# Local queries and keys of the second batch in their own buffers, and one packed product for the third Fourier row tile

## The chip, the cores and the metric

The kernel runs on one core of a Trainium2 chip. The metric is the device time of one execution in microseconds (us). TensorE (PE, with its weight loads as PEld), VectorE (DVE), ScalarE (ACT), GpSimd (POOL) and SyncE (SP) run side by side and wait for each other by semaphores. Most transfers are issued by SP, some by POOL and ACT, and all of them share 16 DMA engines. KB is 1024 bytes.

## The reference

Four batches of 576 tokens with 8 heads of 64 go through four steps, all in float32.

```python
scores = scale * q @ k.T              # heads 0-3: local mask, heads 4-7: strided mask, 32 each
attn = softmax(scores) @ v            # -> x of (4, 576, 512)
mixed = real(fft(fft(x, axis=1), axis=2))
u = x + mixed
x = u + relu(layernorm(u) @ w_ch1) @ w_ch2          # 512 -> 2048 -> 512
u = x + (relu(x.T @ w_tok1) @ w_tok2).T             # over tokens, 576 -> 256 -> 576
out = u + relu(u @ w_ch1b) @ w_ch2b                 # 512 -> 1536 -> 512
```

## The kernel before

**Attention.** The work is 24 groups, six per batch: three local ones (`"l"`, two query tiles of 96 each) and three strided ones (`"s"`). Each group has two halves (`e` = 0 and 1, one parity of heads). `Group.scores` (L193) starts a half with a mask product (L205) and adds the score products (L211). `softmax` (L217) reduces on DVE (L227) and takes exponentials on ACT (L230), `trans` (L234) transposes on PE, `av` (L245) multiplies by the values, and `out` (L257) scales on DVE and stores to the DRAM tensor `xd[b]` from SP (L271, L277, L278).

**Loads.** `load_qk(b, g, pool)` (L170) loads queries and keys of batch `b`, local (`g` = 0) or strided (`g` = 1). Queries go to `qz[g]`, one tile that serves all batches; half of its partitions were set to zero once (L517, L518), so that 128-row products give one head each. Keys go to `k{g}` with one buffer. A load of the next batch thus waits until the scores of the batch before have been taken. Batch 0 is loaded at the start (L514 to L521); the local part of the next batch is asked for at group 3 of each batch (L582), the strided part at its group 0 (L585). SP issues its transfers in one order, and a transfer waits for the eighth one before it on that queue.

**Fourier.** After group 2 of the next batch, `Fourier.load` (L287) fetches the rows of a batch from `xd` in three row tiles (`ST`, 128, 128 and 33 rows): `xa` holds rows from the front half, `xr` their partners from the back half. `prep` (L301) folds them on DVE into `e` (L312 to L316), and ACT and POOL split `e` into a high and a low float32r part in `f` (L317, L318). `s1` (L320) transforms along the tokens: five column tiles, each with high times high, high times low and low times high over the three row tiles, 9 products (6 for the last column). The third tile's rows above 33 are zeros. `s2` (L346) transforms along the channels, adds to `xa` and `xr` (L373) and stores both to `ud[b]` (L375, L376). `fft` (L560) says after which group each piece may go out. The first two batches' Fourier work lies among the attention groups; the third's ends after them, and the fourth's lies in the first steps of the MLP (`last_fft`, L635).

**After it.** `u_rows` (L445) loads token tiles of 128 rows from `ud` for the LayerNorm; the first three are asked for at group 17 (L602), their statistics (L471) at group 19. Then come the first MLP (`gemm1` L413, `gemm2` L432), the token mixer and the second MLP, all led by PE.

**Order.** Up to the second MLP no order is written out by hand: the framework's planner orders each engine's instructions at build, by dependencies, program order and the added hints (`behind`, L74). The constants (L530 to L542) are loaded by POOL's queue and wait for the first batch's strided values (L531).

Of the kernel before, what the change touches and what calls it, by code (L numbers as in the profile page):

```python
# [27 lines left out]
ST = [(0, 128), (128, 128), (256, 33)]  # L28
# [15 lines left out]
def attention_fourier_mlp_kernel(ctx: ExitStack, tc: tile.TileContext, a: dict, out: bass.AP):  # L44
# [118 lines left out]
    k_t, qz = {}, []  # L163
# [6 lines left out]
    def load_qk(b, g, pool):  # L170
        t = pool.tile([P, 2, S], F32, tag=f"k{g}", name="k", bufs=(1, 1)[g])
        k_t[b, g] = t
        for ps in ([slice(0, 1), slice(1, 2)] if b == 0 and g < 1 else [slice(0, 2)]):
            for e in range(2):
                r = slice(64 * e, 64 * e + 64)
                nc.sync.dma_start(out=qz[g][r, e, ps], in_=a["qt"][b, g, r, ps])
            nc.sync.dma_start(out=t[:, ps], in_=a["kt"][b, g, :, ps])
# [7 lines left out]
    class Group:  # L185
# [7 lines left out]
        def scores(self):  # L193
            self.sc, self.mm, self.red = [], [], []
            n, q, k = 2 * self.n, self.q, self.k
            for e in range(2):
# [9 lines left out]
                for i, t in enumerate(self.idx):  # L206
                    qs = slice(96 * t, 96 * t + 96) if self.kind == "l" else slice(SR[t], SR[t] + q)
                    ks = slice(LW[kv(t)], LW[kv(t)] + P) if self.kind == "l" else qs
                    for hp in range(2):
                        j = i * 2 + hp  # L210
                        last = nc.tensor.matmul(  # L211
                            out=sc[:q, j * k:(j + 1) * k], lhsT=qz[self.g][:, e, hp, qs],
                            rhs=k_t[self.b, self.g][:, hp, ks], start=False, stop=j == n - 1)
# [68 lines left out]
    class Fourier:  # L282
# [4 lines left out]
        def load(self, i):  # L287
            r0, n = ST[i]
# [3 lines left out]
            na = min(n, 288 - r0)  # L292
            if i == 2:
                nc.gpsimd.memset(xa[32:33], 0.0)
            if i == 0:
                nc.gpsimd.memset(xr[0:1], 0.0)
            nc.sync.dma_start(out=xa[:na], in_=xd[self.b][r0:r0 + na, :])
            for c0, c1 in ([(1, 16), (16, n)] if i == 0 else [(0, n)]):
                self.last = nc.sync.dma_start(out=xr[c0:c1], in_=xd[self.b][287 + r0 + c0:287 + r0 + c1, :])

        def prep(self, i, prev=None, prev2=None):  # L301
            r0, n = ST[i]
            f = self.f = self.k["f"]
# [13 lines left out]
            behind(nc.scalar.activation(out=f[:n, 0, i], in_=e[:n], func=AF.Copy), prev2)  # L317
            nc.gpsimd.tensor_tensor(out=f[:n, 1, i], in0=e[:n], in1=f32(f[:n, 0, i]), op=ALU.subtract)  # L318

        def s1(self, mt, prev=None):  # L320
            pm = ps_m("g")
            mats = []
            f = self.f
            w = self.k["ss" if mt in (2, 3) else "cs"]
            c = slice(128 * mt, 128 * mt + 128)
# [20 lines left out]
        def s2(self, i, prev=None):  # L346
            r0, n = ST[i]
            c = slice(r0, r0 + n)
# [25 lines left out]
            na = min(n, 288 - r0)  # L374
            nc.sync.dma_start(out=ud[self.b][287 + r0:287 + r0 + n, :], in_=xr[:n])  # L375
            nc.sync.dma_start(out=ud[self.b][r0:r0 + na, :], in_=xa[:na])  # L376
# [10 lines left out]
    class Mlp:  # L387
# [52 lines left out]
        def u_tile(self, c):  # L440
            if c % 3 < 2:
                return self.lp.tile([P, DM], F32, tag="u", name="u", bufs=6)
# [47 lines left out]
    if True:  # L490
# [37 lines left out]
        f = fp.tile([P, 2, 3, 512], F32R, name="f")  # L528
# [3 lines left out]
        for t in (g4[1], alt, f[:, 0, 2], f[:, 1, 2], cs[0][:, 2], cs[1][:, 2], ss[0][:, 2], ss[1][:, 2]):  # L532
            nc.gpsimd.memset(f32(t), 0.0)
        cons = tc.issue_after(tick.ins)
        cons.__enter__()
        for i in range(2):
            for t, w in ((cs[i], a["cs"][i]), (ss[i], a["ss"][i])):
                nc.gpsimd.dma_start(out=t[:, 0:2], in_=w[:, 0:2])
                nc.gpsimd.dma_start(out=t[:33, 2], in_=w[:33, 2])
# [39 lines left out]
        for gno, g in enumerate(gl):  # L579
            b, gi = g.b, g.gi  # L580
            if gi == 3 and b + 1 < B:
                load_qk(b + 1, 0, ap)  # L582
# [18 lines left out]
            if gno == 17:  # L601
                us = [u_rows(T, lp.tile([P, DM], F32, tag="u", name="u", bufs=6)) for T in range(3)]  # L602
            if gno == 21:
                us += [u_rows(T, lp.tile([P, DM], F32, tag="u", name="u", bufs=6)) for T in range(3, 6)]
# [223 lines left out]
        def u_load(T):  # L828
            u = lp.tile([P, DM], F32, tag="u", name="u", bufs=6)
# [211 lines left out]
        def finish(G):  # L1041
# [11 lines left out]
            def halves(t):  # L1053
                if G == Gs[-1]:
                    k = lp.tile([P, DM], F32, tag="u", name="k", bufs=6)
# [87 lines left out]
def _constants():  # L1143
# [15 lines left out]
    s = np.arange(289)  # L1159
    full = {}  # L1160
    for nm, f in (("cs", np.cos), ("ss", np.sin)):
        w = np.zeros((384, 290))
        w[:289, :289] = trig(f, 576, s, s)
        full[nm] = w.reshape(3, P, 290).transpose(1, 0, 2)
# [61 lines left out]
```

## Time and profile before

| what | us |
|---|---|
| median of 3 runs (lowest, highest) | 928.37 (926.74, 932.41) |
| the profiled execution | 922.47 |
| its span | 920.7 |
| PE busy, share of the span | 892.5, 97% |
| DVE, ACT, POOL busy | 560.0, 408.3, 313.0 |

The times are of whole executions; the profile is of one execution, and every row below is from it. Its span starts at its first instruction. Busy times of PE count pipelined matmuls whole, so that they overlap; a busy PE is not PE at its peak. The chain that ended last is 63% PE, 11% DVE and 9% DMA.

### The profile page before, as it was taken

What the parts mean: (1) busy time and instruction counts of PE and PEld (TensorE: products, weight loads), DVE (VectorE), ACT (ScalarE), POOL (GpSimd) and SP (SyncE); (2) the same over time, 40 slices, a digit from 0 to 9 for tenths busy, and PEclk for the clock granted to TensorE, in tenths of its full rate; (3) what the DMA queues carried; (4) which work ended last, traced back from release to release, by engine and by line L of the source; (5) the groups of instructions that cost most, each with busy time, mean ns of one, the idle gap of its engine ahead of it and who ended that gap; (6) DMA issues with size and microseconds to landing.
All of it is one profiled execution on the core that took longest, in us unless ns stands there. A gap on an engine that the chain in (4) does not pass through costs nothing.

```text
span 920.7 us, 15422 instructions
## 1 busy us (share of the span) xinstructions
PE 892.5 (97%) x5554; PEld 824.2 (90%) x5554; DVE 560.0 (61%) x1046; ACT 408.3 (44%) x1069; POOL 313.0 (34%) x372
## 2 busy tenths in 40 slices
PE   7989989999999999999999999999999999999997
PEld 6979988999998989998888897777899999999997
DVE  4667979798894434443443446645434444888774
ACT  5978776353442333233223224323455545444432
POOL 3122222332330133344444333422223001946660
PEclk9989999999999999999999999999999999999999
DMA  9997864234431354644744665579833287156351
GB/s 260 282 289 216 255 205 136 98 127 146 138 111 68 99 160 146 196 128 126 220 141 136 209 200 180 176 262 313 293 120 147 104 270 243 36 161 222 125 203 47
DMA packets 116972, 161.00 MB, mean 175 GB/s; under 512 B 9662, under 2 KB 70180, under 8 KB 116896
## 3 DMA queue, kind: packets, MB, share of 16 engines
q1 hardware_dynamic: 114928, 157.29, 54.0%
q0 software_dynamic: 1712, 2.51, 1.1%
q8 instruction: 44, 0.72, 0.3%
q14 instruction: 32, 0.26, 0.1%
q10 hardware_dynamic: 256, 0.21, 0.1%
HBM read 104.92 MB, written 55.06 MB: 174 GB/s over the span
## 4 chain that ended last, share of the span: by engine, by line
PE 63%; DVE 11%; DMA 9%; ACT 5%; issue 4%; POOL 4%; SPq 3%; POOLq 0%; DVEq 0%; ACTq 0%
PE oo L1036 14%; PE oo L432 10%; PE h L413 10%; PE z L895 8%; PE y L895 4%; DMA wraw<-in_w1b_dram 4%; POOL wt L147 3%; PE tu L806 3%; PE tk L784 3%; PE sc L211 2%; PE w L895 2%; SPq L101 2%; DVE wu L112 2%; DVE wu L108 2%; DVE wu L113 2%
## 5 line engine op out<-in xcount | busy, mean ns | idle before, releaser
L413 PE MATMUL h<-uT,wAh 128*128 128x384 f32 x768 | 203.1, 337 | 0.2
L413 PEld LDWEIGHTS h<-uT,wAh 128*128 128x128 f32 x768 | 139.0, 188 | 5.2 <-PE g L334 0.4
L1036 PE MATMUL oo<-wo,ht 128*128 128x256 f32 x972 | 133.7, 281 | 0.0
L413 PE MATMUL h<-uT,wAl 128*128 128x384 f32 x384 | 129.0, 336 | 0.0
L1036 PEld LDWEIGHTS oo<-wo,ht 128*128 128x128 f32 x972 | 126.5, 189 | 0.0
L432 PE MATMUL oo<-wAh,hh 128*128 128x512 f32 x288 | 113.9, 398 | 4.3 <-ACT hh L417 4.2
L432 PE MATMUL oo<-wAl,hh 128*128 128x512 f32 x288 | 113.7, 395 | 0.0
L432 PE MATMUL oo<-wAh,hl 128*128 128x512 f32 x288 | 104.4, 396 | 0.2 <-DVE hl L418 0.2
L418 DVE SCALAR_TENSOR_TENSOR hl<-h,hh 128x384 fp32r<-128x384 f32 x96 | 52.6, 552 | 76.0 <-ACT hh L417 75.8
L108 DVE TENSOR_SCALAR wu<-wu 128x512 f32<-128x512 f32 (+1 forms) x62 | 38.5, 622 | 78.2 <-ACT wu L106 73.2
L124 POOL TENSOR_TENSOR wAl<-wu,wAh 128x512 fp32r<-128x512 f32 x32 | 45.9, 1437 | 104.3 <-ACT wAh L123 104.3
L417 ACT ACTIVATE hh<-h 128x384 fp32r<-128x384 f32 x96 | 45.9, 484 | 70.4 <-PE h L413 68.9
L147 POOL TENSOR_TENSOR wt<-wu 128x128 f32<-128x128 f32 x48 | 21.1, 461 | 158.3 <-DVE wu L113 158.3
L413 PEld LDWEIGHTS h<-uT,wAl 128*128 128x128 f32 x384 | 72.1, 188 | 2.8
L432 PEld LDWEIGHTS oo<-wAh,hh 128*128 128x128 f32 x288 | 54.1, 188 | 15.6 <-ACT hh L417 6.6
L106 ACT ACTIVATE wu<-wraw 128x512 f32<-128x512 f32 (+1 forms) x62 | 41.0, 662 | 60.6 <-DMA wraw<-in_w1b_dram 46.9
L895 PE MATMUL z<-ut,wo 128*128 128x384 f32 x324 | 64.5, 338 | 1.7 <-DVE ut L863 1.7
L432 PEld LDWEIGHTS oo<-wAh,hl 128*128 128x128 f32 x288 | 53.8, 188 | 13.7 <-DVE hl L418 1.3
L432 PEld LDWEIGHTS oo<-wAl,hh 128*128 128x128 f32 x288 | 54.1, 188 | 8.9
L230 ACT ACTIVATE sm<-sc,st 96x128 f32<-96x128 f32 (+2 forms) x176 | 61.6, 373 | 0.6
L895 PEld LDWEIGHTS z<-ut,wo 128*128 128x128 f32 x324 | 56.4, 188 | 2.1 <-DVE ut L863 2.0
L211 PE MATMUL sc<-k,qz 128*96 128x128 f32 (+2 forms) x352 | 51.0, 283 | 5.3 <-DMA k<-in_kt_dram 5.3
(197 smaller groups left out, 1840.9 us busy)
## 6 DMA issues: line engine op xcount, KB each, us to landing
wo<-wsd SPq DMA_DIRECT2D x84, 256.0 KB
wsd<-wraw SPq DMA_DIRECT2D x24, 448.0 KB
wsd<-wbl SPq DMA_DIRECT2D x24, 448.0 KB
u<-u2d SPq DMA_DIRECT2D x36, 256.0 KB
hd<-hs SPq DMA_DIRECT2D x12, 768.0 KB
hw<-hd SPq DMA_DIRECT2D x36, 256.0 KB
wraw<-in_w1a_dram SPq DMA_DIRECT2D x16, 512.0 KB
wraw<-in_w2a_dram SPq DMA_DIRECT2D x16, 512.0 KB
```

The source lines that it names most:

```text
L106: behind(nc.scalar.activation(out=f32(u), in_=f32(high), func=AF.Abs, scale=2.0**16), relu.get("hh"))
L108: clamp = eng().tensor_scalar(f32(u), f32(u), E_MIN, E_MAX, op0=ALU.max, op1=ALU.min)
L124: nc.gpsimd.tensor_tensor(out=lo[:, :n], in0=u, in1=f32(hi[:, :n]), op=ALU.subtract)
L147: nc.gpsimd.tensor_tensor(out=o, in0=x, in1=y, op=ALU.add if plus else ALU.subtract)
L211: last = nc.tensor.matmul(out=sc[:q, j * k:(j + 1) * k], lhsT=qz[self.g][:, e, hp, qs], rhs=k_t[self.b, self.g][:, hp, ks], start=False, s ...
L230: self.exp = nc.scalar.activation(out=smv[:, j, :], in_=sc[:, j, :], func=AF.Exp, scale=SCALE, bias=st[:, 1, j:j + 1], accum_out=st[:, 2, ...
L413: nc.tensor.matmul(out=h[:, :384], lhsT=l[:, ws], rhs=r[:, kd, :], start=x == 0, stop=x == 11)
L417: relu["hh"] = nc.scalar.activation(out=hh, in_=h[:, :384], func=AF.Relu)
L418: relu["hl"] = nc.vector.scalar_tensor_tensor(out=hl, in0=h[:, :384], scalar=0.0, in1=f32(hh), op0=ALU.max, op1=ALU.subtract)
L432: nc.tensor.matmul(out=self.o[c][i], lhsT=l[:, s], rhs=r, start=first and x == 0, stop=last and x == 2)
L895: Unit.last = nc.tensor.matmul(out=bank[:, :384], lhsT=w[:, c + kd * P:c + kd * P + P], rhs=r[:, kd], start=first and x == 0, stop=x == 5, ...
L1036: nc.tensor.matmul(out=acc[G][bank][:, 256 * half:256 * half + 256], lhsT=lh[:, i], rhs=w[:, c:c + 256], start=m == 0 and x == 0 and half ...
```

## The change

Four tiles `qo[e, hp]` take the second batch's local queries, one for each parity and head pair, with their other half set to zero. They come out of the pool of the LayerNorm tiles `u`, whose buffers grow from 512 to 576 columns. `k0` has two buffers. The second batch's local load is asked for right after the first batch's loads, and the third batch's at group 3 of the first batch; nothing is loaded there at group 3 of the second.

In the Fourier stage the rows are numbered anew: row tiles 0 and 1 hold rows 1 to 256, the third holds rows 288, 257 to 287 and 0, with the partners alike (`rows`). The third tile's high part stands on partitions 0 to 32 of a tile `f3`, its low part on 64 to 96, and a second copy of 32 high rows on 96 to 127. The tables carry the matching parts, so that one product does what three did. Row 0 and row 288 have a low part of zero in the tables, so partition 96 may hold the low part. Each of the third tile's row sets moves in three pieces, to and from DRAM.

```diff
-        t = pool.tile([P, 2, S], F32, tag=f"k{g}", name="k", bufs=(1, 1)[g])
+        t = pool.tile([P, 2, S], F32, tag=f"k{g}", name="k", bufs=(2, 1)[g])
+        own = b == 1 and g == 0
...
+                if own:
+                    for hp in range(2):
+                        nc.sync.dma_start(out=qo[e, hp][r], in_=a["qt"][b, g, r, hp])
+                else:
+                    nc.sync.dma_start(out=qz[g][r, e, ps], in_=a["qt"][b, g, r, ps])
...
+            for t, p0, r0, n in self.rows(i):
+                self.last = nc.sync.dma_start(out=t[p0:p0 + n], in_=xd[self.b][r0:r0 + n, :])
+
+        def rows(self, i):
+            xa, xr = self.x[i]
+            if i < 2:
+                return (xa, 0, 1 + 128 * i, 128), (xr, 0, 288 + 128 * i, 128)
+            return ((xa, 32, 0, 1), (xa, 1, 257, 15), (xa, 16, 272, 16),
+                    (xr, 0, 575, 1), (xr, 1, 544, 15), (xr, 16, 559, 16))
...
+            h, l = (f[:, 0, i], f[:, 1, i]) if i < 2 else (f3[0:33], f3[64:97])
+            behind(nc.scalar.activation(out=h, in_=e[:n], func=AF.Copy), prev2)
+            if i == 2:
+                behind(nc.scalar.activation(out=f3[96:128], in_=e[0:32], func=AF.Copy), prev2)
+            nc.gpsimd.tensor_tensor(out=l, in0=e[:n], in1=f32(h), op=ALU.subtract)
...
-            for i in range(3):
+            for i in range(2):
+                h, l = f[:, 0, i, c], f[:, 1, i, c]
                 if mt < 4:
-                    h, l = f[:, 0, i, c], f[:, 1, i, c]
-                    mats += [(h, w[0][:, i], m), (h, w[1][:, i], m), (l, w[0][:, i], m)]
+                    mats += [(h, w[:, i], m), (h, w[:, 2 + i], m), (l, w[:, i], m)]
                 else:
-                    mats += [(f[:, :, i, 256], w[0][:, i], 2), (f[:, 0, i, 256:257], w[1][:, i], 1)]
+                    mats += [(f[:, :, i, 256], w[:, i], 2), (h, w[:, 2 + i], 1)]
+            mats.append((f3[:, c], w[:, 4], 128 if mt < 4 else 1))
...
+            for t, p0, r0, k in self.rows(i)[::-1]:
+                nc.sync.dma_start(out=ud[self.b][r0:r0 + k, :], in_=t[p0:p0 + k])
...
+        for e in range(2):
+            for hp in range(2):
+                qo[e, hp] = lp.tile([P, S], F32, tag="u", name="qo", bufs=6)
+                nc.vector.memset(qo[e, hp][64 - 64 * e:128 - 64 * e], 0.0)
         load_vl(0)
         load_qk(0, 1, ap)
         vlast = load_vs(0)
+        load_qk(1, 0, ap)
-
-        cs = [fp.tile([P, 3, 290], F32R, name=f"cs{i}") for i in range(2)]
-        ss = [fp.tile([P, 3, 290], F32R, name=f"ss{i}") for i in range(2)]
+        cs, ss = (fp.tile([P, 5, 290], F32R, name=nm) for nm in ("cs", "ss"))
...
             if gi == 3 and b + 1 < B:
-                load_qk(b + 1, 0, ap)
+                if b != 1:
+                    load_qk(2 if b == 0 else 3, 0, ap)
                 load_vl(b + 1)
```

## Rows read from the trace of the kernel before

**Rows 1.** The page: busy us, share and instructions of each engine.

```profile
PE 892.5 (97%) x5554; PEld 824.2 (90%) x5554; DVE 560.0 (61%) x1046; ACT 408.3 (44%) x1069; POOL 313.0 (34%) x372
```

**Rows 2.** Busy time by stretches; the last three columns: PEclk, DMA share, GB/s.

```profile
8.00:42.00 34.00, 33.82 (x303) 31.89 (x303) 18.86 (x43) 29.21 (x153) 7.23 (x14) 1.00 1.10 306
30.00:42.00 12.00, 12.00 (x116) 11.58 (x115) 8.87 (x21) 11.37 (x60) 2.60 (x5) 1.00 1.15 320
42.00:46.00 4.00, 4.00 (x43) 3.91 (x41) 1.94 (x5) 3.94 (x20) 0.00 (x0) 1.00 0.41 129
...
60.00:64.00 4.00, 4.00 (x19) 3.85 (x20) 1.50 (x6) 0.82 (x3) 0.00 (x0) 0.50 1.04 411
64.00:68.00 4.00, 4.00 (x33) 3.93 (x32) 3.48 (x8) 2.30 (x14) 1.29 (x1) 0.78 1.04 253
62.00:148.00 86.00, 80.19 (x683) 75.75 (x681) 72.76 (x175) 64.69 (x269) 23.65 (x18) 0.96 0.71 219
...
120.00:122.00 2.00, 1.53 (x7) 0.93 (x8) 1.91 (x10) 1.82 (x10) 0.00 (x0) 0.59 0.43 149
122.00:124.00 2.00, 2.00 (x12) 1.92 (x11) 1.79 (x9) 1.54 (x7) 0.00 (x0) 0.56 0.76 245
```

**Rows 3.** PE's timeline: start us, us, operation, count, [idle before <- releaser].

```profile
31.10 0.46 PE L205 MATMUL sc<-mask_l,ident_r 96*96 96x512 f32 x1
...
35.13 0.46 PE L205 MATMUL sc<-mask_l,ident_r 96*96 96x512 f32 x1
...
55.02 0.46 PE L205 MATMUL sc<-mask_l,ident_r 96*96 96x512 f32 x1
...
59.83 0.50 PE L211 MATMUL sc<-k,qz 128*96 128x128 f32 x1 [4.36 <-DMA k<-in_kt_dram]
...
66.92 0.39 PE L205 MATMUL sc<-mask_l,ident_r 96*96 96x512 f32 x1
```

**Rows 4.** Timeline of the SP queue, 0 to 150 us.

```profile
19.80 0.58 SPq L177 DMA_DIRECT2D k<-in_kt_dram  x1
...
30.66 0.58 SPq L177 DMA_DIRECT2D k<-in_kt_dram  x1
...
42.81 0.75 SPq L278 DMA_DIRECT2D xd<-x  x1
...
52.98 0.57 SPq L177 DMA_DIRECT2D k<-in_kt_dram  x1
```

**Rows 5.** SP's waits from 42 to 46 us, and PE's timeline at 43 us.

```profile
SPq L278 <- DMA k<-in_kt_dram: 1.0, 1, 1.0
...
43.25 1.04 PE L211 MATMUL sc<-k,qz 128*126 128x126 f32 x8
```

**Rows 6.** Transfers by line: count, KB each.

```profile
qz<-in_qt_dram SPq DMA_DIRECT2D x14, 288.0 KB
k<-in_kt_dram SPq DMA_DIRECT2D x7, 576.0 KB
...
cs<-in_cs_dram POOLq DMA_DIRECT2D x2, 290.0 KB, 11.1
```

**Rows 7.** The chain that ended last, 150 to 160 us: start us, us, what.

```profile
152.73 2.42 PE g L334 x18
```

**Rows 8.** Groups by line, 0 to 230 us: busy us, mean ns, idle before.

```profile
L317 ACT ACTIVATE f<-e 33x512 fp32r<-33x512 f32 x4 | 2.5, 628 | 1.1 <-DVE e L316 1.1
```

**Rows 9.** The memsets by line (0 to 230 us), and DVE's timeline.

```profile
L518 DVE MEMSET qz<- 64x576 f32 x4 | 2.2, 538 | 0.7 <-issue 0.7
...
10.93 1.52 DVE L227 TENSOR_REDUCE st<-sc 96x4 f32<-96x512 f32 x2 [4.41 <-PE sc L211]
```

**Rows 10.** Timeline of SP and DVE, 104 to 126 us.

```profile
109.96 0.46 SPq L376 DMA_DIRECT2D ud<-xa  x1
...
111.79 0.32 SPq L447 DMA_DIRECT2D u<-ud  x1
...
116.50 0.69 DVE L471 BATCH_NORM_STATS2 bs<-u 128x6 f32<-128x512 f32 x1 [2.57 <-DMA u<-ud]
```

More of the change, by code (lines that the diff above doesn't have):

```diff
@@ L27 @@
 LW = [max(0, 96 * t - 32) for t in range(6)]
[L28 removed]
+NR = (128, 128, 33)
 SN = [7, 7, 6, 6, 6]
@@ L211, in scores @@
                         last = nc.tensor.matmul(
-                            out=sc[:q, j * k:(j + 1) * k], lhsT=qz[self.g][:, e, hp, qs],
+                            out=sc[:q, j * k:(j + 1) * k], lhsT=(qo[e, hp] if (self.b, self.g) == (1, 0) else qz[self.g][:, e, hp])[:, qs],
                             rhs=k_t[self.b, self.g][:, hp, ks], start=False, stop=j == n - 1)
@@ L291, in load @@
             self.x[i] = xa, xr
-            na = min(n, 288 - r0)
             if i == 2:
[L294 to L299, printed above, removed]
+                nc.gpsimd.memset(xa[0:1], 0.0)
+                nc.gpsimd.memset(xr[32:33], 0.0)
+            for t, p0, r0, n in self.rows(i):
[6 more added lines that the diff above has]
+                    (xr, 0, 575, 1), (xr, 1, 544, 15), (xr, 16, 559, 16))
         def prep(self, i, prev=None, prev2=None):
-            r0, n = ST[i]
-            f = self.f = self.k["f"]
+            n = NR[i]
+            f, f3 = self.k["f"]
             xa, xr = self.x[i]
@@ L441, in u_tile @@
             if c % 3 < 2:
-                return self.lp.tile([P, DM], F32, tag="u", name="u", bufs=6)
+                return self.lp.tile([P, S], F32, tag="u", name="u", bufs=6)[:, :DM]
             return self.pool.tile([P, DM], F32, tag="v", name="v", bufs=3)
@@ L527, in attention_fourier_mlp_kernel @@
         alt = fp.tile([P, 258], F32R, name="alt")
-        f = fp.tile([P, 2, 3, 512], F32R, name="f")
+        f = fp.tile([P, 2, 2, DM], F32R, name="f"), fp.tile([P, DM], F32R, name="f3")
         g4 = [fp.tile([P, 290], F32R, name=f"g4{x}") for x in "hl"]
@@ L535, in attention_fourier_mlp_kernel @@
         cons.__enter__()
+        for t, nm in ((cs, "cs"), (ss, "ss")):
+            nc.gpsimd.dma_start(out=t, in_=a[nm])
         for i in range(2):
-            for t, w in ((cs[i], a["cs"][i]), (ss[i], a["ss"][i])):
-                nc.gpsimd.dma_start(out=t[:, 0:2], in_=w[:, 0:2])
-                nc.gpsimd.dma_start(out=t[:33, 2], in_=w[:33, 2])
             nc.gpsimd.dma_start(out=cd[i], in_=a["cd"][i])
@@ L601, in attention_fourier_mlp_kernel @@
             if gno == 17:
-                us = [u_rows(T, lp.tile([P, DM], F32, tag="u", name="u", bufs=6)) for T in range(3)]
+                us = [u_rows(T, lp.tile([P, S], F32, tag="u", name="u", bufs=6)[:, :DM]) for T in range(3)]
             if gno == 21:
-                us += [u_rows(T, lp.tile([P, DM], F32, tag="u", name="u", bufs=6)) for T in range(3, 6)]
+                us += [u_rows(T, lp.tile([P, S], F32, tag="u", name="u", bufs=6)[:, :DM]) for T in range(3, 6)]
             if gno == 19:
@@ L828, in u_load @@
         def u_load(T):
-            u = lp.tile([P, DM], F32, tag="u", name="u", bufs=6)
+            u = lp.tile([P, S], F32, tag="u", name="u", bufs=6)[:, :DM]
             nc.sync.dma_start(out=u, in_=u2d[T // 9][T % 9])
@@ L1054, in halves @@
                 if G == Gs[-1]:
-                    k = lp.tile([P, DM], F32, tag="u", name="k", bufs=6)
+                    k = lp.tile([P, S], F32, tag="u", name="k", bufs=6)[:, :DM]
                     nc.scalar.activation(out=k, in_=t, func=AF.Copy)
@@ L1157, in trig @@
         return v
-    s = np.arange(289)
+    s = np.concatenate([np.arange(1, 257), [288], np.arange(257, 288), [0]])
+    for nm, f in (("cs", np.cos), ("ss", np.sin)):
+        w = np.zeros((289, 290))
+        w[:, :289] = trig(f, 576, s, s)
+        h, l = _split(w)
+        t = np.zeros((P, 5, 290), np.float32)
+        t[:, 0:2], t[:, 2:4] = (x[:256].reshape(2, P, 290).transpose(1, 0, 2) for x in (h, l))
+        t[0:33, 4], t[64:97, 4], t[97:128, 4] = h[256:], h[256:], l[257:288]
+        c[nm] = t
     full = {}
[L1161 to L1164, printed above, removed]
     d, k = np.arange(256), np.arange(257)
```

19 lines of the change are left out of this document (6 added, 13 removed).

## The prediction

> **What bounds the kernel now.** I read the page's engine shares first. PE is busy for 97% of the span [rows 1], but PE's busy time counts matmuls that overlap, so I split the span with the table by stretches [rows 2]. From about 148 us to the end PE works without a gap worth naming: a matmul taken away there shortens the end. The first 148 us are different. There DMA, PE, ACT and DVE hand work to each other: from 62 to 148 us none is full (PE 80.2, DVE 72.8, ACT 64.7 of 86 us), and from 30 to 42 us the DMA engines are (share 1.15, 320 GB/s; 1.10 over 8 to 42), after which they fall to 0.41 [rows 2]. So I read PE's timeline next. One mask product begins each half group. In the second batch two halves take 35.13 - 31.10 = 4.0 us. The third batch begins at 55.02, its scores wait 4.36 us to 59.83, and its third half begins only at 66.92: 11.9 us for two halves [rows 3]. Three Fourier products sit between, 0.134 us each [rows 7], 0.8 us at half clock. The pause costs 11.9 - 4.0 - 0.8 = 7.1 us, more than itself, because the granted clock is 0.50 from 60 to 64 and 0.78 from 64 to 68 us [rows 2]: PE had stood idle and came back at the lower level, 1.2 GHz.
>
> Why that load is late: the timeline of the SP queue shows its k issued only at 52.98, behind the first batch's stores and row loads; the second batch's strided k was issued at 30.66 [rows 4]. At 42.81 SP issues a store [rows 4], and for the k it had waited 1.0 us [rows 5]. That store is the eighth transfer after the k, so this is where the strided k landed. Its first scores start at 43.25 [rows 5]. The margin there is 0.44 us.
>
> **The change part by part.** *The pause at 59.83.* The third batch's local load moves to where the second batch's stands now (k at 19.80 [rows 4]): it waits only for the first batch's scores. Its pause goes: -7.1 us.
>
> *What is late next.* The bytes are not fewer, they come sooner. Ahead of the second batch's strided load there now lie both the second and the third batch's local loads: two q of 288 KB and one k of 576 KB more [rows 6], 1152 KB. The cosine and sine tables grow by 140 KB (2 x 725 KB by the diff's shape, against 4 x 290 [rows 6] and 4 x 37.4, which is 33 rows of 290 words). That is 1.32 MB in a stretch in which DMA is full: at 320 GB/s, 4.1 us [rows 2]. At most 1.0 us comes back, since five strided stores that went out beside it (at most 63 rows of 256 words, 63 KB each) now queue behind it. The strided k then lands at 45.9 to 46.9 against a need at 43.25: a wait of 2.7 to 3.7 us. I take 3.2. PE takes its work in order, so the values' products and transposes of the last local group stand behind the waiting scores, ACT's copies and exponentials behind those. The clock falls as before: the 4.36 us pause cost 2.7 us beyond itself, and a shorter gap near 119 us also left 0.59 in 120 to 122 [rows 2]. So +5.9 us, bounds 0 (the data comes in time) and 7.1 (a pause as long as the one that goes). Swap: -7.1 + 5.9 = -1.2.
>
> *The packed third tile.* In each batch four column tiles go from 9 to 7 products and the last from 6 to 5: 9 products fewer, 36 in all, 290 columns each. 18 of them took 2.42 us on the chain: 0.134 us each [rows 7]. From 152.73 us on, where PE sets the end, stand 24 of the third batch's products (18 + 6) and the fourth's 42; of those 14 go: -1.9 us. The other 22 (2.9 us) lie in the coupled stage, where DVE works 72.8 of 86 us beside PE; bounds 0 and -2.9, I take a third, -1.0.
>
> *Additions.* One ACT copy of 32 rows per batch: the copy of 33 rows takes 0.628 us [rows 8]. Three fall in the stage where ACT is 75% busy, one under PE work; bounds 0 and 2.5, I take 0.6. Four memsets on DVE (four now take 2.2 us and 0.7 of issue) fit into the 4.41 us in which DVE waits for its first scores [rows 9]: nothing, and at most 2.9 us if they were put behind them. The POOL memsets that go were idle filler.
>
> *The stores and the LayerNorm loads.* The third tile now goes out in six pieces and row 0 of the batch in the last of them, so the first token tile's load no longer goes ahead of the third row tile. Now: the store at 109.96 releases the load at 111.79, 1.83 us later, and DVE waits 2.57 us for it until 116.50 [rows 10]. Three pieces instead of one, at an issue of 0.32 to 0.46 us [rows 10], put that load some 1 us later, and the statistics of an earlier tile (0.69 us) fall behind the wait. Bounds 0 and 3.0 (all six pieces ahead, plus 0.7); I take 1.5, since DVE already idles there and PE with it. The extra three loads per batch cost SP 1.2 us, and the third tile is read last: covered.
>
> The Trainium skill speaks against this piece: its page "DMA: Bandwidth & Descriptors" (Rules for kernel authors) says small transfers should be joined, since under 64 KB one pays mostly overhead, and (Anatomy of one DMA) puts a fixed part of about 2.0 us on each. An estimate by that page, with six pieces one after another instead of two, would be 8 us more per batch. The row agrees with the size (1.83 us from issue to use), but an issue holds SP for 0.32 to 0.46 us only, so pieces overlap, and the sum goes by that.
>
> Sum: -1.2 - 1.9 - 1.0 + 0.6 + 1.5 = -2.0 us. The profiled execution took 922.47 us, so 920.5 by its own clock. It lies 5.9 us under the median of the runs shown (928.37, from 926.74 to 932.41); moved with it, **926.4 us**.
>
> **Rivals.** *The data comes in time.* If the ring serves the second batch's strided load before the bytes added, or the planner puts that load earlier, no new pause appears: -7.1 - 1.9 - 1.0 + 0.6 + 1.5 = -7.9, so 920.5 us. For it: the margin of 0.44 us shows the transfer was just sufficient. Against it: DMA ran full from 8 to 42 us and dry just after, which is what landing by total bytes looks like.
>
> *Slower: the LayerNorm loads.* If all six pieces and the statistics stand ahead, DVE waits 3.0 us longer at 116, PE's gap near 119 grows with it and the low clock after it (0.59 and 0.56 over 4 us [rows 2] cost 1.7) comes in full a second time: +4.7 instead of +1.5, so -2.0 + 3.2 = +1.2, 929.6 us. It decides the sign from the point where this term passes 3.5 us. For it: DVE is in order, already waits there, and the chain runs through it. Against: the planner may set other DVE work before the statistics. By the Trainium skill's page named above it would be 8 us per batch; the short issues speak against that.
>
> *It does not do what it says.* SP takes its queue in order, and a transfer also waits for the eighth before it; with five more at the start the third batch's load could still leave late. Then the old pause stays and none is added: -1.9 - 1.0 + 0.6 + 1.5 = -0.8, 927.6 us.
>
> **How the numbers follow.** Forecast 0.50 (its own range 922 to 931: the swap between -4 and 0, the other bounds, the spread of the runs), data in time 0.25, slower 0.15, not as said 0.10. The range 918.5 to 934.0 takes in the better half of the second case and the slower one with the spread of the runs. One per cent is 9.3 us, about what a measurement of this kernel tells from no change. Faster by more than that needs the pause gone and most of the hidden products paid: 0.14. Slower by more needs the slower rival and a new order of the early stage besides: 0.05. The rest is within: 0.81.
>
> **What would show it.** Right: no wait for k at the third batch's local scores; a new wait of 2.7 to 3.7 us at the first 126-row scores of the second batch, near 43 us, with a granted clock of about 0.5 behind it; the third batch's third half near 65 to 66 us; 33 stage-1 products per batch; DVE's wait for `u` longer than 2.57 us. Wrong: no PE wait near 43 us with DMA full through it, or both pauses, or an end of the attention stage that moves by more than 5 us either way.

## The result and the profile after

The changed kernel is slower, where 2.0 us faster was forecast. Its median is 932.64 us (930.57 to 940.01, 14 runs) beside 925.12 us for the kernel before on the same chips (921.09 to 932.41, 14 runs): ratio 1.0082, 95% interval 1.0056 to 1.0108, so 7.5 us. The profiled execution took 934.57 us (span 932.5), 11.8 us of span more than before; the two profiled executions lie on opposite sides of their medians, so the traces overstate the loss by 4.6 us (934.57 - 932.64 and 925.12 - 922.47).

The page shows the products that are gone (5554 instructions on PE before [rows 1]) and no less time for them:

```profile
PE 894.7 (96%) x5518; PEld 825.6 (89%) x5518; DVE 564.2 (61%) x1050; ACT 410.7 (44%) x1073; POOL 314.6 (34%) x361
```

The time is lost before PE takes the lead. The first product of the first MLP starts at 157.76 us instead of 147.52, 10.2 us later; from there to the end the changed kernel needs 774.7 us, the one before 773.2. I follow the loss along the mask products, one for each half group (a half is one parity of heads of a group). PE's timeline of the changed kernel:

```profile
43.41 0.74 PE L210 MATMUL sc<-mask_l,ident_r 96*96 96x512 f32 x1 [0.54 <-ACT sm L235]
47.30 1.51 PE L258 MATMUL av<-vl,pt 128*96 128x64 f32 x8 [1.44 <-DMA vl<-in_vl_dram]
51.02 0.77 PE L210 MATMUL sc<-mask_s,ident_r 126*126 126x504 f32 x1
...
64.65 0.46 PE L210 MATMUL sc<-mask_l,ident_r 96*96 96x512 f32 x1
65.74 0.47 PE L210 MATMUL sc<-mask_l,ident_r 96*96 96x512 f32 x1
69.16 0.40 PE L210 MATMUL sc<-mask_l,ident_r 96*96 96x512 f32 x1
```

The third batch begins at 64.65 (55.02 before) and its third half at 69.16 (66.92 before) [rows 3]: no wait for `k` there any more, 4.5 us for two halves instead of 11.9, as predicted. But a new pause stands ahead of it, in the second batch. Stretches of the changed kernel (the same columns as [rows 2]):

```profile
36.00:40.00 4.00, 2.94 (x29) 2.69 (x27) 0.45 (x2) 1.65 (x10) 0.00 (x0) 1.00 1.18 309
40.00:44.00 4.00, 2.93 (x15) 2.39 (x16) 2.36 (x6) 2.35 (x12) 0.00 (x0) 0.66 1.10 378
44.00:48.00 4.00, 2.56 (x14) 2.24 (x12) 1.98 (x5) 1.88 (x11) 0.00 (x0) 0.50 0.96 232
48.00:52.00 4.00, 4.00 (x25) 3.99 (x24) 0.69 (x1) 2.51 (x14) 0.00 (x0) 0.50 0.38 122
```

PE is short of work from 36 us, some seven us sooner than I had placed the pause, and runs at 1.2 GHz (0.50) from 44 to 52 us. From the second batch's first half to its second strided one PE needs 23.6 us (31.43 to 55.01) instead of 14.0 (31.10 to 45.07): the new pause costs 9.6 us. The one exchanged for the other leaves +2.2 us at 69.16.

The rest comes at the LayerNorm. SP's timeline (first fence), DVE's (second), and PE's longest wait there and its first MLP product (third) of the changed kernel; then the same two of the kernel before (fourth). The rows answer to [rows 10].

```profile
110.61 0.42 SPq L188 DMA_DIRECT2D vs<-in_vs_dram  x1
111.15 0.36 SPq L101 DMA_DIRECT2D wraw<-in_w1a_dram  x1
111.60 1.15 SPq L387 DMA_DIRECT2D ud<-xa  x2
112.84 1.10 SPq L387 DMA_DIRECT2D ud<-xr  x3
113.99 0.25 SPq L387 DMA_DIRECT2D ud<-xa  x1
116.27 0.77 SPq L282 DMA_DIRECT2D xd<-x  x1
118.52 0.75 SPq L283 DMA_DIRECT2D xd<-x  x1
119.38 1.35 SPq L458 DMA_DIRECT2D u<-ud  x3
```

```profile
122.20 0.69 DVE L482 BATCH_NORM_STATS2 bs<-u 128x6 f32<-128x512 f32 x1 [6.41 <-DMA u<-ud]
...
130.91 0.16 DVE L469 TENSOR_SCALAR nr<-mv 128x3 f32<-128x3 f32 x1
...
153.19 0.17 DVE L489 SCALAR_TENSOR_TENSOR mv<-mv 128x3 f32<-128x3 f32 x1
```

```profile
124.24 1.37 PE L346 MATMUL g<-cs,f 128*2 128x290 f32 x5 [5.73 <-DVE gl L356]
...
157.76 1.17 PE L424 MATMUL h<-uT,wAh 128*128 128x384 f32 x3 [0.69 <-ACT uT L413]
```

```profile
120.47 1.61 PE L334 MATMUL g<-cs,f 128*2 128x290 f32 x6 [1.77 <-DVE gl L344]
...
147.52 1.39 PE L413 MATMUL h<-uT,wAh 128*128 128x384 f32 x3
```

SP's waits of the changed kernel, 109 to 120 us:

```profile
SPq L282 <- DMA vs<-in_vs_dram: 2.0, 1, 2.0
SPq L283 <- DMA wraw<-in_w1a_dram: 1.5, 1, 1.5
```

All three token tiles are loaded in one go at 119.38; before, DVE had two of them by 111.25 us and the third was issued at 111.79. The six pieces of the third tile stand ahead of them, and these fill SP's queue: `vs`, `wraw` and the six are eight transfers, so the strided store behind them waits 2.0 us for `vs` and the next one 1.5 us for `wraw`, and the three loads stand behind both. DVE stops for 6.41 us (2.57 before). PE stops behind it, 5.73 us for `gl` until 124.24 (1.77 until 120.47 before), and the granted clock is 0.50 from 124 to 130 us (0.59 and 0.56 from 120 to 124 before [rows 2]). DVE's chain of small instructions for the inverse root, 117.90 to 123.93 before, now runs from 130.91 to 153.36, strewn among the Fourier work of two batches; from 132 to 152 us DVE has no gap left (4.00 of 4 us in each stretch). The last mask product is only 2.65 us late (140.91 against 138.26), the first MLP product 10.2.

### The profile page after: what moved, and what is told of

It reads as the page before. It is cut to its first block, busy times and chain, and to the rows that moved or that the text cites. A ratio compares the mean times of both kernels' runs of the same rounds, so it can differ in the third digit from the quotient of the medians.

```text
span 932.5 us, 15377 instructions
## 1 busy us (share of the span) xinstructions
PE 894.7 (96%) x5518; PEld 825.6 (89%) x5518; DVE 564.2 (61%) x1050; ACT 410.7 (44%) x1073; POOL 314.6 (34%) x361
## 3 DMA queue, kind: packets, MB, share of 16 engines
q0 software_dynamic: 1168, 2.65, 1.0%
## 4 chain that ended last, share of the span: by engine, by line
PE 39%; DVE 6%; DMA 6%; POOL 3%; SPq 3%; issue 3%; ACT 3%; DVEq 0%; POOLq 0%; ACTq 0%
PE oo L1051 14%; PE z L910 8%; PE y L910 4%; PE tu L821 3%; DMA wraw<-in_w1b_dram 3%; POOL wt L147 3%; PE tk L799 3%; SPq L101 2%; PE oo L443 2%; PE w L910 2%; PE h L424 2%; DVE wu L108 1%; DVE wu L112 1%; DVE wu L113 1%; ACT wraw L153 1%
## 5 line engine op out<-in xcount | busy, mean ns | idle before, releaser
L113 DVE SCALAR_TENSOR_TENSOR wu<-wraw,wu 128x512 int32<-128x512 int32 (+1 forms) x62 | 48.2, 779 | 1.0
```

What stands on the lines that cost most here:

```text
L113: v.scalar_tensor_tensor(out=u, in0=low, scalar=29, in1=u, op0=ALU.logical_shift_right, op1=ALU.bitwise_or)
```

## The experiments

All ratios are against the kernel before on the same chip. My theory when they were planned: the packed tile's row order makes the loss, by the late LayerNorm loads (the second rival of the prediction, priced too low), and the moved loads only shift a pause. The rival: the early loads fill the DMA queue and make the loss, and the late LayerNorm follows from it.

**One part alone.** First the loads, on the kernel before:

```diff
+        if own:
+            t = k_t[b, g] = [fp.tile([P, S], F32, tag=x, name="k", bufs=1) for x in ("xa0", "xr0")]
...
+                qo[e, hp] = fp.tile([P, S], F32, tag=("xa", "xr")[e] + str(1 + hp), name="qo", bufs=1)
...
+        load_qk(1, 0, ap)
...
-                load_qk(b + 1, 0, ap)
+                if b != 1:
+                    load_qk(2 if b == 0 else 3, 0, ap)
```

> Only the moved loads, with the Fourier stage as before (the four query tiles and the second batch's local keys lie in buffers of the second batch's Fourier rows, which are not in use yet; the keys come in two transfers). If the packed third tile's row order is the cause of the loss, the time is within 3 us of the kernel before (ratio 0.997 to 1.003), the pause at the third batch's local scores is gone and one near 40 to 50 us takes its place, and the first MLP product starts within 3 us of before (147.5 us). If the early loads are the cause, this kernel carries the loss: 5 to 10 us slower than before (1.005 to 1.011).

Measured: 1.0015 (0.9994 to 1.0037), 927.40 us. No loss shows here; the interval ends at 3.4 us. PE's timeline of this run, and four of its stretches:

```profile
47.55 1.11 PE L222 MATMUL sc<-k,qz 128*126 128x126 f32 x8 [2.76 <-DMA xd<-x]
...
64.60 0.39 PE L216 MATMUL sc<-mask_l,ident_r 96*96 96x512 f32 x1
...
89.59 0.38 PE L371 MATMUL fa<-alt,g4h 128*128 128x258 f32 x1 [1.79 <-ACT g4h L353]
```

```profile
44.00:48.00 4.00, 1.24 (x12) 0.96 (x11) 0.69 (x1) 4.00 (x20) 0.14 (x1) 1.00 0.69 224
48.00:52.00 4.00, 4.00 (x43) 3.93 (x41) 2.13 (x6) 2.55 (x12) 1.13 (x1) 1.00 0.29 68
...
92.00:96.00 4.00, 4.00 (x21) 3.91 (x20) 4.00 (x12) 2.78 (x13) 0.22 (x1) 0.50 0.82 281
96.00:100.00 4.00, 4.00 (x20) 3.85 (x20) 4.00 (x8) 3.61 (x15) 2.58 (x2) 0.50 0.92 239
```

This is the exchange that I had forecast, but for the clock: a wait of 2.76 us at the second batch's first strided scores (the profile puts it down to a store, which these scores don't read; of what they read the `k` of that load was issued last, at 33.48 instead of 30.66, and SP's eighth transfer behind it, the store at 47.43, waited 0.5 us for it), and the third batch's third half at 64.60, 2.3 us sooner than before. The granted clock stays at 1.00 behind that wait, where I had forecast some 0.5. The gain does not last. At 89.59 PE waits 1.79 us for the last column tile, works at 1.2 GHz to 100 us, and the first MLP product comes at 147.80, where it came before.

Then the packed tile, with the loads as before:

```diff
-        load_qk(1, 0, ap)
...
-                if b != 1:
-                    load_qk(2 if b == 0 else 3, 0, ap)
+                load_qk(b + 1, 0, ap)
```

> Only the packed third tile, loads as before. If its row order is the cause, this kernel carries the loss: 5 to 9 us slower than before (1.005 to 1.010), with the LayerNorm loads issued after all stores of the first batch's third tile (near 119 us instead of 112) and the first MLP product 7 to 10 us later than 147.5. If the early loads are the cause, the 36 products that are gone show: 0 to 3 us faster than before (0.997 to 1.000) and the LayerNorm loads not later than 114 us.

Measured: 1.0081 (1.0054 to 1.0108), 934.34 us, the whole loss. The LayerNorm loads are issued at 118.94. DVE's and PE's timelines of this run:

```profile
121.80 0.70 DVE L482 BATCH_NORM_STATS2 bs<-u 128x6 f32<-128x512 f32 x1 [6.24 <-DMA u<-ud]
```

```profile
156.22 1.41 PE L424 MATMUL h<-uT,wAh 128*128 128x384 f32 x3 [0.69 <-ACT uT L413]
```

The packed tile makes the loss without the moved loads, and the rival falls.

**The row order.** The changed kernel with the third tile first:

```diff
-            for i in range(3):
-                p = (n + 7 + (i + d + 1) // 2, (i + d + 1) % 2)
+            for x, i in enumerate((2, 0, 1)):
+                p = (n + 7 + (x + d + 1) // 2, (x + d + 1) % 2)
...
-            for i in {7: (0, 1, 2)}.get(x, ()):
+            for i in {7: (2, 0, 1)}.get(x, ()):
```

> The changed kernel, but the channel transform (s2) takes the third row tile first, then the first and the second, so that row 0 and rows 257 to 287 of the batch go out first and the first token tile no longer waits for the last stores. If the packed tile's row order is the cause, 5 to 9 us come back (926 to 928 us beside 932.6 of the changed kernel, or 1.000 to 1.003 of before). If the early loads are the cause, nothing does (1.007 to 1.010 of before).

Measured: 1.0012 (0.9994 to 1.0029), 927.98 us: the loss comes back but for a rest. DVE's timeline, and PE's longest wait and first MLP product in this run:

```profile
117.46 1.33 DVE L482 BATCH_NORM_STATS2 bs<-u 128x6 f32<-128x512 f32 x2 [5.63 <-DMA u<-ud]
...
138.28 0.15 DVE L489 SCALAR_TENSOR_TENSOR mv<-mv 128x3 f32<-128x3 f32 x1
```

```profile
122.22 1.37 PE L346 MATMUL g<-cs,f 128*2 128x290 f32 x5 [5.53 <-DVE gl L356]
...
150.09 0.41 PE L424 MATMUL h<-uT,wAh 128*128 128x384 f32 x1 [0.23 <-DVE uT L414]
```

DVE still waits 5.63 us, but until 117.46 instead of 122.20. The chain ends 15 us sooner and no longer decides when the MLP starts: 150.09 instead of 157.76. PE's stop is nearly as long as in the changed kernel (5.53 us for 5.73, again with a clock of 0.50 behind it), so that stop by itself is not what the MLP is late by. The same order with the loads left as before:

> The packed third tile with its rows going out first, and the loads as before. If the row order was all that was wrong with the packed tile, this is the kernel before less 36 products: 0 to 3 us faster than before (0.997 to 1.000). If the joined tables (725 KB in one transfer, all seven of the constants' transfers issued in one go near 21 to 24 us instead of up to 33 us) cost something of their own, by holding up the second batch's keys near 33 us and the third batch's near 60 us, it is 1 to 4 us slower than that: 1.000 to 1.004.

Measured: 1.0029 (1.0004 to 1.0054), 928.36 us. The order is worth 1.0081 - 1.0029, some 5 us, but even so the packed tile does not pay. Not all of the 5 us lies at the LayerNorm in these two executions: the mask product that starts at 95.86 before starts at 98.14 with the packed tile alone and at 95.86 with its rows first.

**The third batch's load later.** It was asked for behind the second batch's strided load:

```diff
                 load_qk(b, 1, ap)
                 load_vs(b)
+                if b == 1:
+                    load_qk(2, 0, ap)
```

> The changed kernel, but the third batch's local load is asked for at the start of the second batch, behind that batch's strided load and values, instead of at group 3 of the first batch. If the packed tile's row order is the cause, the early stage gets better by 1 to 3 us and the end by no more (1.005 to 1.009 of before). If the early loads are the cause, 5 to 8 us come back (1.000 to 1.003), with the second batch's strided queries issued near 28 us again, and no gap of DVE behind stores near 35 us.

Measured: 1.0074 (1.0046 to 1.0102). On the question it says nothing: the planner issued this load at 23.05 to 24.76 us all the same (22.83 to 24.72 in the changed kernel). But it shows the loss without a shift ahead of it: the mask product that starts at 95.86 before starts at 95.77 here. DVE's and PE's timelines of this run:

```profile
119.73 0.69 DVE L482 BATCH_NORM_STATS2 bs<-u 128x6 f32<-128x512 f32 x1 [6.53 <-DMA u<-ud]
```

```profile
121.77 1.37 PE L346 MATMUL g<-cs,f 128*2 128x290 f32 x5 [5.83 <-DVE gl L356]
...
154.45 1.41 PE L424 MATMUL h<-uT,wAh 128*128 128x384 f32 x3 [0.69 <-ACT uT L413]
```

The MLP starts 6.9 us late here, all of it behind 96 us. PE comes back no later than with the third tile first (121.77 and 122.22), and still the MLP starts 4.4 us after that run's; DVE comes back 2.3 us after it (119.73 and 117.46), and its chain ends at 150.04 instead of 138.43.

**Where the chain stands.** If the strewn chain were the cause, moving it forward should help. First a hint that held a score maximum behind it:

```diff
                 g.softmax(e)
+                if gno == 22 and e == 0:
+                    behind(g.red[0], stats["last"])
```

> The changed kernel with one hint more: on DVE the score maxima of the last batch's fifth group come behind the last instruction of the first LayerNorm statistics. In the changed kernel the 13 small instructions of that chain lay scattered from 130.9 to 153.2 us among other DVE work; before, they took 117.9 to 123.9. If the delay of the loads itself costs the time, nothing comes back (1.006 to 1.010 of before). If it is the place that the planner gives the chain once its data is late, the chain ends near 133 us, the first MLP product comes near 150 us instead of 157.8, and 6 to 8 us come back (0.999 to 1.003).

Measured: 1.0082 (1.0053 to 1.0111). The hint moved the maximum to 142.98, behind a chain that was as strewn as before and ended at 143.07, and PE stood idle from 140 to 144 us; the test was a poor one. So a second hint held back Fourier work alone:

```diff
-            behind(nc.vector.tensor_tensor(out=wv, in0=pairs, in1=cross, op=ALU.add), prev)
+            behind(nc.vector.tensor_tensor(out=wv, in0=pairs, in1=cross, op=ALU.add), stats.get("last") if self.b == 2 else prev)
...
+            if gno == 19:
+                mvs = ln_stats(us, lp, g.red[1])
             while slices and slices[0][0] <= min(gno, 22):
```

> The changed kernel, third tile last as there, with a better hint than in the run that held the score maxima back: the first LayerNorm statistics stand ahead of the Fourier pieces in the program, and on DVE the Fourier stage's own work (the second batch's results, the third batch's folds) comes behind the chain's last instruction, no score work. If the loss is made by the chain's 13 small instructions being strewn among that work, the chain ends near 137 us instead of 153, the first MLP product comes at 149 to 152 us instead of 157.8, and 4 to 7 us come back (1.001 to 1.004 of before). If the late loads themselves make it, by the stop of DVE and PE near 117 to 123 us, or if the Fourier work only becomes late in its turn, the time stays (1.006 to 1.010).

Measured: 1.0084 (1.0056 to 1.0112), 932.42 us. DVE's timeline and PE's of this run:

```profile
136.80 0.16 DVE L491 SCALAR_TENSOR_TENSOR mv<-mv 128x3 f32<-128x3 f32 x1
```

```profile
154.97 0.85 PE L348 MATMUL g<-cs,f 128*128 128x290 f32 x2 [4.71 <-POOL f L331]
155.62 1.19 PE L426 MATMUL h<-uT,wAh 128*128 128x384 f32 x3
```

The chain ends at 136.96 and the MLP still starts at 155.62. Now the third batch's folds are late, and the products that read them stand ahead of the MLP in PE's order. So moving the chain gives nothing back: DVE is full from 136 to 152 us, and whatever is put last there holds PE. The test is not clean: DVE stood still for 7.58 us ahead of the statistics here, and for 0.9 us from 132 to 136, where the changed kernel has no gap. Whether another order of the same work would gain is not shown. What did help was the sooner load.

**Late loads and small pieces, each on the kernel before.** Nothing is packed here:

```diff
-                us = [u_rows(T, lp.tile([P, DM], F32, tag="u", name="u", bufs=6)) for T in range(3)]
+                us = {T: u_rows(T, lp.tile([P, DM], F32, tag="u", name="u", bufs=6)) for T in (2, 0, 1)}
+                us = [us[T] for T in range(3)]
```

> The kernel before, nothing packed and no load moved, but the three LayerNorm loads are asked for in the order third, first, second token tile, so that SP has all three behind the third row tile's stores, as the packed tile's row 0 does. If the lateness of these loads alone makes the loss, this kernel is slower by 4 to 8 us (1.004 to 1.009), with DVE waiting 5 us or more for the first tile near 116 us. If the loss needs what else the packed tile brings (six pieces, joined tables, the shift of 2 us that is there by 98 us), it is within 2 us (0.998 to 1.002).

Measured: 1.0023 (0.9997 to 1.0050). DVE's wait is 2.57 us as before, but ends at 118.58, and the chain ends at 133.52, 9.6 us later than before; the first MLP product comes at 148.28, 0.8 us later. Less than expected. But DVE does not stand longer here than before, so this run tests loads that are 2.1 us later, and not the longer stop. Such loads cost little, as long as the chain still ends before the attention does.

```diff
-            nc.sync.dma_start(out=ud[self.b][287 + r0:287 + r0 + n, :], in_=xr[:n])
-            nc.sync.dma_start(out=ud[self.b][r0:r0 + na, :], in_=xa[:na])
+            for d, t, k in ((287 + r0, xr, n), (r0, xa, na)):
+                for c0, c1 in ((0, 1), (1, 16), (16, k)) if i == 2 else ((0, k),):
+                    nc.sync.dma_start(out=ud[self.b][d + c0:d + c1, :], in_=t[c0:c1])
```

> The kernel before, with the third row tile stored in six pieces (1, 15 and the rest of the rows, twice) instead of two; row order and loads as they were. If small pieces by themselves cost time, 2 to 6 us slower (1.002 to 1.006); by my estimate in the prediction, 1 us; if the order is what counts, within 1.5 us (0.999 to 1.002).

Measured: 1.0045 (1.0023 to 1.0068), 928.10 us: 4 us for six pieces instead of two in each of four batches. The profiled execution, the fastest of the twelve (925.13), does not show where: its first MLP product is at 145.98, sooner than before. That stays open.

**Fewer pieces.** Third tile first, rows 257 to 287 in one piece of 31 instead of 15 and 16; the first of the two also has the late tables (below):

```diff
-            return ((xa, 32, 0, 1), (xa, 1, 257, 15), (xa, 16, 272, 16),
-                    (xr, 0, 575, 1), (xr, 1, 544, 15), (xr, 16, 559, 16))
+            return ((xa, 32, 0, 1), (xa, 1, 257, 31),
+                    (xr, 0, 575, 1), (xr, 1, 544, 31))
```

> Third tile first and tables late, with each of the third tile's row sets in two pieces (1 and 31 rows) instead of three (1, 15 and 16 rows): per batch two loads and two stores fewer. If the number of small transfers costs time beside their order, the first LayerNorm loads come 0.5 to 1 us sooner than 114.6 us and the time falls by 1 to 3 us (0.995 to 0.998 of before). If it is the order alone, there is no change (0.997 to 1.001).

Measured: 1.0178 (1.0140 to 1.0215), 942.71 us, by far the slowest. SP's timeline (first fence), POOL's (second) and PE's (third) of this run:

```profile
99.19 0.69 SPq L388 DMA_DIRECT2D ud<-xa  x2
```

```profile
108.76 0.52 POOL L298 MEMSET xa<- 1x512 f32 x1 [8.60 <-DMA ud<-xa]
109.35 1.26 POOL L330 TENSOR_TENSOR f<-e,f 33x512 fp32r<-33x512 f32 x1
```

```profile
110.66 0.61 PE L347 MATMUL g<-cs,f 128*128 128x290 f32 x1 [5.37 <-POOL f L330]
```

The store of 31 rows and of one is issued by 99.88; POOL's zeroing of a row for the next batch waits until 108.76 for it, 8.9 us. Behind it in POOL's order stands the low part of `f`, and PE waits 5.37 us for that. In the run that differs from this one by the pieces alone (late tables, 15 and 16 rows) the low part stands ahead of the zeroing, so POOL's order has a share in that wait. Late tables or not makes no difference:

> Third tile first, tables at their old place, each of its row sets in two pieces (1 and 31 rows). The same pieces with late tables gave 1.0178, against 0.9987 with 1, 15 and 16 rows. If a store of 31 rows is slow in itself (8.9 us from the issue at 99.9 to the end of POOL's wait at 108.8 there), this kernel loses as much: 12 to 18 us slower than before (1.013 to 1.019). If it was the late tables that made the difference, it is within 3 us of the run with the third tile first (0.999 to 1.005).

Measured: 1.0184 (1.0158 to 1.0210).

**The tables later.** Third tile first, and the tables asked for when the second batch's strided keys have landed:

```diff
-        tick = nc.gpsimd.memset(f32(g4[0]), 0.0)
...
+        def constants(klast):
+            tick = nc.gpsimd.memset(f32(g4[0]), 0.0)
...
-                load_qk(b, 1, ap)
+                klast = load_qk(b, 1, ap)
+                if b == 1:
+                    constants(klast)
```

> As the run with the third tile first, but the Fourier tables are asked for only when the second batch's strided keys have landed (near 43 us) instead of the first batch's strided values (near 22 us); 2.4 MB leave the stretch from 22 to 42 us. If the tables' bytes are what holds up the second batch's values and strided load there, the granted clock stays at 1.00 from 40 to 56 us, and 2 to 5 us come back against the run without it (0.996 to 0.999 of before). If the pause there comes from the moved loads alone, or costs nothing at the end, there is no change (1.000 to 1.003).

Measured: 0.9987 (0.9959 to 1.0014), 924.76 us. PE's timeline and stretches of this run:

```profile
59.03 1.94 PE L259 MATMUL av<-vs,pt 126*126 126x64 f32 x8 [4.42 <-DMA vs<-in_vs_dram]
```

```profile
56.00:60.00 4.00, 0.97 (x5) 1.00 (x5) 0.00 (x0) 1.58 (x10) 0.00 (x0) 0.79 1.01 309
60.00:64.00 4.00, 4.00 (x22) 4.00 (x22) 0.15 (x1) 0.00 (x0) 0.00 (x0) 0.50 0.97 344
```

The clock stays at 1.00 until 56 us, and then the pause is there again, for the strided values this time. The interval overlaps that of the third tile first with early tables, so a gain by the late tables is not shown. With the hint that failed above, with the one of the chain, and with the loads alone:

> As the run before it, with the statistics held together by the hint as well. With the third tile first the chain still ends at 138.4 us. If its place matters only when it is later than the attention's last products (near 148 us), this changes nothing against the run without the hint (within 1 us); if an earlier end also helps, up to 2 us come back.

Measured: 1.0010 (0.9988 to 1.0033).

> Third tile first, tables late, and the chain ahead of the Fourier work on DVE. If the end of the chain (138.4 us with the third tile first) is no longer late, this gives nothing against the run with tables late (within 1.5 us of it, 0.997 to 1.001 of before). If the second token tiles or the first MLP still wait for it, 1 to 3 us come back (0.994 to 0.997).

Measured: 1.0010 (0.9988 to 1.0031); the chain ends at 127.95 and the first MLP product is at 148.15.

> The moved loads without the packed tile, with the tables asked for when the second batch's strided keys have landed. The loads alone gave 1.0015: the old pause gone, one of 2.76 us at the second batch's strided scores in its place. If bytes ahead of that load make the new pause, it is gone here with 2.3 MB less in the way, and the gain that was expected of the loads shows: 3 to 7 us faster than before (0.992 to 0.997). If SP's queue and not the bytes holds the strided load back, the pause stays and the time is that of the loads alone (1.000 to 1.003).

Measured: 1.0013 (0.9989 to 1.0037): the pause comes at 52 to 56 us instead (PE busy for 2.23 of 4 us, clock 0.58 in 56 to 60). Of all versions only the one with the third tile first and late tables has a median under that of before, and its interval holds no change. Neither hint adds a gain to it.

## Why the prediction was wrong

*The old pause goes (-7.1) and a new one comes (+5.9).* With the loads alone the wait was right (2.76 us where 2.7 to 3.7 was forecast, at the scores named), and the clock was not: it stayed at 1.00, so that the new pause cost 3.0 us (44.32 to 49.44, for 42.94 to 45.07 before). The old one gave back 6.6 (59.26 to 64.60, for 55.02 to 66.92), and 1.4 had been lost ahead of both (44.32 for 42.94). That the exchange gave -2.3 at 64.60 (forecast -1.2), within its bounds, is thus in part luck. I had not seen that it is given back at 89.59, so that the loads are worth nothing at the end (1.0015).

In the whole change the old pause gave back 7.4 us, but the new one cost 9.6, more than its bound of 7.1, and its place was wrong: the values came late (a wait of 1.44 us until 47.30), and PE was short of work from 36 us. I counted the bytes ahead of the strided load, and not that the joined tables go out at once: seven transfers, issued from 22.76 to 26.5 us, where before thirteen were issued in two bursts until 33.2 us. With the third tile first, late tables agree: the first strided half of the second batch starts at 42.93 with them and at 51.14 without. The joined tables alone do not make it each time: with the loads as before that half (42.94 before) came at 46.68 in one run and at 43.12 in the other. Nor did stores give way to the strided load: with the loads alone seven went out between its `k` and that one's landing (35.29 to 46.20), and seven had gone out before (31.71 to 41.00), not five as I counted.

Why no version escapes is, as I read it, in the row of the DMA engines: from 5 to 65 us their share is 1.02 before (first row) and 0.99 with the loads moved (second row), so that a load that goes sooner makes another late. The stretch from 5 to 65 us of the kernel before and of the run with the loads alone:

```profile
5.00:65.00 60.00, 54.27 (x461) 50.70 (x462) 33.85 (x80) 46.80 (x233) 14.15 (x23) 0.95 1.02 291
```

```profile
5.00:65.00 60.00, 54.84 (x480) 51.68 (x481) 35.59 (x84) 47.24 (x233) 13.42 (x23) 1.00 0.99 285
```

*The products (-1.9 and -1.0).* From the first MLP product on, the packed kernels need 776.4 us (packed tile alone) and 776.0 us (third tile first), the ones without it 776.6 us (loads alone) and 776.1 us (late LayerNorm loads). That the profiled execution of before has 773.2 us there, with the same code as the last of these, says how far one execution may lie. Over all runs it is 773.2 to 777.4 us without the packed tile and 773.6 to 778.0 with it: no run shows the -1.9, nor the -1.0 ahead of it. Six pieces alone cost 0.45%, the packed tile with its rows first 0.29%, so the products may be worth some 1.5 us; the intervals do not fix it, and the two kernels differ in more than the products.

*The additions (+0.6).* ACT is busy for 2.4 us more (410.7 and 408.3), within the bound of 2.5; what of it reaches the end is not shown.

*The stores and the LayerNorm loads (+1.5, bounds 0 to 3.0).* This is the step that failed. The packed tile alone cost 7.5 us (0.81% of 926), its products and additions taken in, and its first MLP product came 8.7 us late (156.22). Two things were mis-sized. I priced a piece by its issue (0.32 to 0.46 us) and let pieces overlap; six pieces alone cost 4 us (where is open), and together with `vs` and `wraw` they fill the eight places of SP's queue, so that the loads leave at 119.38, 5.1 us after the last piece. I had named that limit of eight in the rival that the change does not do what it says, and did not apply it here. And I ended the sum at DVE's wait: 3.84 us more of it (6.41 - 2.57) became some 8 us at the MLP (10.2 less the 2.2 that were there by 69 us), and in the run with the third batch's load asked for later 3.96 us more (6.53 - 2.57) became 6.9. I read the cause from the traces: what follows is a stretch in which DVE has no idle time to give, and the chain that ends in it decides when the MLP starts. That the order of the rows makes most of the loss is shown by the runs with the third tile first; why a longer stop grows so is not tested by itself.

*The rivals.* The one that decided was the one on the other side, the LayerNorm loads, at 0.15: right in its place and in its mechanism as far as the wait, PE's longer gap and the low clock behind it go, wrong in its price (929.6; the median moved by 7.5 us, which is 935.9 by the clock of the runs shown then). That the median of 932.64 lies inside the stated range is luck: the kernel before measured 925.12 this time, and 928.37 then. The argument against it, that the planner may set other DVE work before the statistics, failed: DVE stood still for 6.41 us. Of the other two rivals neither came: the data was late, and the old pause went. The Trainium skill's page "DMA: Bandwidth & Descriptors" (Rules for kernel authors) pointed the right way: small transfers should be joined. The 8 us per batch I had worked out from a figure that the page gives for transfers issued by GpSimd, and SP issues these pieces; six pieces alone cost 4 us in all four batches, so the sign was right and the size was not.

*What it would show.* The old wait gone, 36 products fewer, DVE's wait longer than 2.57: right. The wait near 43 us and the third half at 65 to 66: near enough with the loads alone (2.76 us until 47.55, and 64.60), but without the clock of 0.5, and not so in the whole change. The last mask product moved by 2.65 us only, but the first MLP product, at which the forecast's coupled stage ends, by 10.2: more than the 5 us that I had named as the sign of an error.

## What to carry to other kernels

When a change renumbers rows, follow each row to its reader: one row that moves into the last tile makes every tile that reads it wait for the last store. Here 3.8 to 4.0 us of added wait became 7 to 8 us behind a stretch with a full engine, so a wait that is added ahead of one is to be priced at the first point behind it where PE sets the end, and not at the wait. Where DMA is full throughout, ask which load a moved load will make late, and split a change that has two parts before it is judged.

## What had not been expected of the hardware

Stores of 31 rows of 2 KB took far longer than one of 32. With 32 rows (the run with late loads on the kernel before) the store issued at 110.84 has let POOL's zeroing go by 112.69:

```profile
110.84 0.40 SPq L376 DMA_DIRECT2D ud<-xa  x1
```

```profile
112.69 0.52 POOL L294 MEMSET xa<- 1x512 f32 x1 [7.49 <-DMA ud<-xa]
```

That is 1.85 us from the start of its issue, against 8.9 us from the end of the issue above and 10.0 us in the second run with 31 rows (issued by 105.96, waited for until 115.95). It is not that the DMA engines were full. A stretch of the first run with 31 rows, while POOL waits for the store:

```profile
107.00:109.00 2.00, 0.00 (x0) 0.00 (x0) 0.98 (x3) 0.26 (x2) 0.24 (x1) 0.69 0.07 26
```

The share of the 16 engines is 0.07, about one of them, at 26 GB/s; from 101.5 to 103.5 us it is 0.07 too. By an estimate from that row the store's 62 KB take 2.4 us, so most of the 8.9 us went by before its rows moved. The Trainium skill's page "DMA: Bandwidth & Descriptors" (Why a DMA increments its semaphore by 16 and not by 1) has a rule for it: a transfer is spread over the largest number of engines, up to 16, that divides the slowest dimension of both its sides, so 31 rows go to one engine and 32 to all 16. The share of 0.07 agrees. By that rule 15 and 16 rows go to 15 and to 16 engines, and as two pieces they were better than 31 as one (1.0012 and 1.0184 with early tables), against the rule on joining small transfers.

And a short wait can cost far more than itself: 1.79 us at 89.59 in the run with the loads alone was followed by 8 us at 1.2 GHz, while in the changed kernel a wait of 1.77 us at 94.17 (PE busy for 2.23 of 4 us in 92 to 96) left the clock at 2.4 GHz, and so did the 2.76 us at 47.55 in the run with the loads alone (1.24 of 4 us in 44 to 48). In these rows the length of a wait alone does not tell which it will be; what does is open.
